# Two attention chunks turned by VectorE instead of TensorE, and an ordered start of the x sums, in a fused RetNet and GELU kernel on Trainium2

## The chip, the cores and the metric

The kernel runs on one core of a Trainium2 chip. Five engines work side by side, each through its own list of instructions in order: TensorE (PE), VectorE (DVE), ScalarE (ACT), GpSimd (POOL) and SyncE (SP). Here SP only issues loads and a few stores, POOL computes and issues transfers of its own, and all transfers share 16 DMA engines. The metric is the device time of one execution in microseconds, and a lower one is better. "Span" is the time from the first to the last instruction of the one execution that was profiled.

## What is computed

```python
def _attn_ref(q, k, v):                       # 4 batches, 8 heads, 768 steps, head size 64
    gamma = 1.0 - 2.0 ** (-5.0 - np.arange(H, dtype=np.float32))
    scale = 1.0 / np.sqrt(D)
    for t in range(S):
        state = gamma[None, :, None, None] * state + np.einsum('bhd,bhe->bhde', k[:, :, t], v[:, :, t])
        y[:, :, t] = scale * np.einsum('bhd,bhde->bhe', q[:, :, t], state)
    return y

def _moe_ref(x, w_in, w_out):                 # 3072 x 512, 512 x 2048, 2048 x 512
    h = x @ w_in
    g = h * (1.0 / (1.0 + np.exp(-1.702 * h)))
    return (g @ w_out).astype(np.float32)
```

The attention's output, heads side by side, is the x of the two products. The two weights come as float64 and everything is computed in float32.

## The kernel before

**Blocks.** The attention is cut into chunks of 64 steps. One "chunk" j covers two batches at once, one in each half of the 128 partitions, so there are 12 chunks for each pair of batches and 24 in all. Four chunks make a block of 512 tokens, and there are six blocks, 0 to 5. A block goes through the first product (up, L405 to L426 for blocks 0 and 1, L463 from block 2 on), GELU on ACT, and the second product (down, L670, or down49, L551). From block 2 on, the first product uses sums of x and of the weights that save multiplications.

**One chunk.** `load` (L124) fetches q, k and v. `turn` (L238) transposes q and k. `attend` (L279) writes the matmuls on PE: the inner products of chunk j into the tile pa, and for an earlier chunk f the state's update (also in pa), the part that comes from the state, and the part within the chunk (both in py). pa and py exist once each in PSUM. `masked` (L314) multiplies the inner products with the decay mask on DVE, `decay` (L261) scales k, `aged` (L349) scales the old state, `updated` (L360) adds the new part, `by_state` (L319) and `output` (L331) write x, in block 1 into X1.

**Two ways to turn.** Chunks 0 to 7 (`j < 2 * CB`) are loaded plainly, by two DMAs of 128 KB for each of q, k and v, and turned by PE: 16 matmuls against a unit matrix (L248), which ACT copies from PSUM (L259). Their decays and agings are done head by head on ACT (L270, L355). Chunks from 8 on are loaded as squares: eight DMAs of 32 KB for each of q and k (L154), which put 32 x 32 blocks in place so that one transpose on DVE (L251) for each of q and k finishes the work. They also need k and v as they are, in four DMAs of 64 KB each (L140). Their decays and agings are single instructions on POOL (L272, L357). The two ways lay heads out differently over the halves of the partitions. So `halves_anew` (L791) once rewrites the mask, the decays and the state between chunk 7 and chunk 8; it is called from `late_loads` (L786), the first loads for chunks 8 and 9.

**The raw weights.** Each of the 16 weight pieces w0 to w15 arrives as two DMAs of 512 KB (L177, "w5a", "w5b") in one of three raw buffers (L166), taken in turn: w7 waits until w4 is converted, and so on. Conversion is one instruction on ACT (`start`, "abs", L204), three on DVE (`half`) and three more (`rest`). W0 to w7 serve the first product, w8 to w15 the second.

**The order.** Up to the end of block 1's first product the order is written by hand, as a list of names (L844 to L861). The list interleaves loads ("q6"), turns, steps ("step6-5" is `attend(6, 5)`), conversions, the units of block 0's first product ("up0.0.3": token half 0, weight piece 3), those of block 1 ("up1.8"), and their GELUs ("gate"). PE follows it to the letter, and so does every instruction made under `pin` or `keep_in_program_order`, on its own engine and against other such instructions. Instructions that are not pinned are placed by a scheduler. That holds for most of POOL's work.

**Around the block boundaries.** `sums_x` (L437) makes four differences of x in place on POOL: X4 = X2 − X0, X6 = X3 − X2, X5 = X3 − X4 and X2 = X1 − X5. It is called once in each of blocks 1 to 4 for the block that follows (L908). The first product of the next block wants X0, X1, X5, X4, X6, X3 and X2, in this order. Block 1's results go through `put` (L681): DVE adds into a tile o, of which there are two, and POOL issues its transfer to DRAM (L684, pinned). In the later blocks POOL does four additions per tile first (L600 to L603) and then issues it (L604).

Of the kernel before, what the change touches and what calls it, by code (L numbers as in the profile page):

```python
# [13 lines left out]
P = 128  # L14
# [14 lines left out]
def kernel(  # L29
# [32 lines left out]
    B, H, S, D = q.shape  # L62
# [56 lines left out]
        return tc.keep_in_program_order(i) if ordered[0] else i  # L119


    QKV = {}

    def load(j, what="qkv"):  # L124

        b, c = j // NC * 2, j % NC
        rows = slice(c * D, (c + 1) * D)
        keep = tc.keep_in_program_order if j < 2 * CB else lambda i: i  # L130

        def plain(name, src, tag, bufs, engine=sp):
            t = two.tile([P, H, D], F32, name=name + "_in", tag=tag, bufs=bufs)
            QKV[name, j] = t
            for i in range(2):
                if j < 2 * CB:
                    keep(engine.dma_start(t[i * D:(i + 1) * D], src[b + i, :, rows, :].rearrange("h p d -> p h d")))  # L137
                else:
                    for r in range(2):
                        keep(engine.dma_start(t[r * D:(r + 1) * D, i * HP:(i + 1) * HP],  # L140
                                              src[b + i, r * HP:(r + 1) * HP, rows, :].rearrange("h p d -> p h d")))

        if j < 2 * CB:
            if "q" in what:
                plain("q", q, "q_sq", 2)
            if "k" in what:
                plain("kn", k, "k_sq", 2, sp if j else act)
        elif "q" in what:
            for name, src in (("q", q), ("k", k)):
                t = two.tile([P, H, D // C4, C4], F32, name=name + "_sq")  # L150
                for r0 in range(0, P, C4):
                    for n in range(D // C4):
                        t0 = c * D + n * C4
                        tc.keep_in_program_order(sp.dma_start(  # L154
                            t[r0:r0 + C4, :, n], src[b + r0 // D, :, t0:t0 + C4, r0 % D:r0 % D + C4]
                            .rearrange("h p d -> p h d")))
                QKV[name, j] = t
        if "v" in what:
            if j >= 2 * CB and c < NC - 1:
                plain("kn", k, "kn", 1)  # L160
            plain("v", v, "v", 2)

# [65 lines left out]
    def home(j, name):  # L228

        at = ["qT", "kT", "kd", "at"].index(name)  # L230
        shape = [[HP, P] if j < 2 * CB else [H, D]] * 2 + [[H, D], [2, HP, D]]
        shape = shape[at]
        if j >= 2 * CB:
            return one.tile([P] + shape, F32, name=name, tag=name, bufs=[2, 1, 1, 2][at])
        t = G[:, at, j % 2 * 2:j % 2 * 2 + 2].rearrange("p s t -> p (s t)")
        return t.rearrange("p (a b c) -> p a b c", a=2, b=HP) if at == 3 else t.rearrange("p (a b) -> p a b", a=shape[0])

    def turn(j):  # L238

        QT[j], KT[j] = home(j, "qT"), home(j, "kT")  # L240
        if j < 2 * CB:

            x = QKV.pop(("q", j)), QKV["kn", j]
            TURNED[j] = p = [ps.tile([P, HP, P], F32, name="pt", tag="y") for i in range(2)]
            for n in (1, 0) if j else (0, 1):
                for s in range(HP):
                    for r in range(2):
                        pe.matmul(p[n][HALF[r], s, :], x[n][:, HP * r + s, :], ident, start=True, stop=True)  # L248
        else:
            for t, name in ((QT[j], "q"), (KT[j], "k")):  # L250
                tc.keep_in_program_order(dve.transpose(  # L251
                    t.rearrange("p h t -> p (h t)"), QKV.pop((name, j)).rearrange("p h n d -> p (h n d)")))
        if 2 * CB <= j < NCH - 2:
            load(j + 2, "qk")
# [6 lines left out]
    def decay(j):  # L261

        if j % NC == NC - 1:
            return
        KD[j] = home(j, "kd")
        x = QKV["kn", j]
        if j < 2 * CB:

            for h in range(H):
                pin(act.activation(KD[j][:, h], x[:, h], AF.Copy, scale=cold[:, H + h:H + h + 1]))  # L270
        else:
            pool.tensor_mul(KD[j].rearrange("p (i s) d -> p i s d", i=2), x.rearrange("p (i s) d -> p i s d", i=2),  # L272
                            cold[:, None, H:H + HP, None].to_broadcast([P, 2, HP, D]))

    def by_half(t, j):

        return t.rearrange("p s (w t) -> p w s t" if j < 2 * CB else "p (w s) t -> p w s t", w=2)

    def attend(j, f=None):  # L279

# [7 lines left out]
        if f is not None:  # L288
# [17 lines left out]
            for s2 in range(2):  # L306
                for u in range(2):
                    for w, o in TWO:
                        s = 2 * s2 + o
                        pe.matmul(py[HALF[o], w, 0, 2 * u + s2 if f < 2 * CB else 2 * s2 + u, :],  # L310
                                  vn[HALF[w], HP * u + s, :], a[HALF[w], u, s, :], start=True, stop=True)
            PU[f], PY[f] = pa[:, :, 1], py

    def masked(j):  # L314
        AT[j] = home(j, "at")
        pin(dve.tensor_mul(AT[j], PA.pop(j)[:, :, 0],
                           mask if j < 2 * CB else mask[:, 0:1].to_broadcast([P, 2, HP, D])))

    def by_state(f):  # L319

        if f < 2 * CB:
            SHARE[f] = tmp = two.tile([P, 2, 4, D], F32, name="tmp", bufs=1)
            pin(dve.tensor_mul(tmp.rearrange("p i a t -> p i (a t)").rearrange("p i (r t) -> p i r t", r=2),
                               PY[f][:, :, 1].rearrange("p r (i s) t -> p i r (s t)", i=2),
                               rowd.rearrange("p (r s) t -> p r (s t)", r=2)[:, None].to_broadcast([P, 2, 2, P])))
        else:
            SHARE[f] = tmp = two.tile([P, 4, 2, D], F32, name="tmp", bufs=1)
            pin(dve.tensor_mul(tmp.rearrange("p a i t -> p i a t"), PY[f][:, :, 1],
                               rowd[:, None].to_broadcast([P, 2, HP, D])))

    def output(f):  # L331
# [1 line left out]
        th, t0 = f % CB // 2, f % 2 * D  # L333
        x = (X1 if f // CB == 1 else X)[:, 2 * th:2 * th + 2]
        y = PY.pop(f)[:, :, 0]
        if f < 2 * CB:
            x = x.rearrange("p r s (i t) -> p (r s) i t", i=2)[:, :, :, t0:t0 + D]
            y = y.rearrange("p i a t -> p a i t")
            b = "p i a t -> p a i t"
# [2 lines left out]
            b = "p (r s) i t -> p r (s i) t"  # L342
        if c:
            tmp = SHARE.pop(f)
            pin(dve.tensor_add(x, y, tmp.rearrange(b) if f < 2 * CB else tmp.rearrange(b, r=2)))  # L345
        else:
            pin(act.activation(x, y, AF.Copy))

    def aged(f):  # L349

        c = f % NC
        old, new = state[c % 2], state[(c + 1) % 2]
        if f < 2 * CB:
            for s in range(HP):
                pin(act.activation(new[:, :, s], old[:, :, s], AF.Copy, scale=whole[:, s:s + 1]))  # L355
        else:
# [78 lines left out]
        pool.tensor_sub(w[2], w[1], w[5])  # L435

    def sums_x():  # L437
        pool.tensor_sub(X[:, 4], X[:, 2], X[:, 0])
        pool.tensor_sub(X[:, 6], X[:, 3], X[:, 2])
        pool.tensor_sub(X[:, 5], X[:, 3], X[:, 4])  # L440
        pool.tensor_sub(X[:, 2], X[:, 1], X[:, 5])
# [344 lines left out]
    def late_loads():  # L786
        load(2 * CB, "qkv")
        load(2 * CB + 1, "qk")
        halves_anew()

    def halves_anew():  # L791

# [1 line left out]
                                        ap=[[0, P], [1, H]]))  # L794
        pool.tensor_copy(mask[HALF[1], 0], mask[HALF[1], 1])
        pool.tensor_copy(cold[HALF[1], H:H + HP], cold[HALF[1], H + HP:2 * H])
        old, new = state[2 * CB % NC % 2], state[(2 * CB + 1) % NC % 2]
        for u in range(2):
            pool.dma_start(new[HALF[1 - u], u], old[HALF[u], 1 - u])
        for u in range(2):  # L800
# [5 lines left out]

        "mask": lambda: pin(dve.tensor_mul(m3, products["rows"], cold[:, 0:H, None].to_broadcast([P, H, D]))),
        "causal": causal, "rows": rows,
        "rowd": lay_rowd, "whole": lay_whole, "late_loads": late_loads,
        "warm": keep_warm}  # L810
    for j in range(2 * CB):
        for name in "qkv":
# [31 lines left out]
    for name in """  # L844
# [2 lines left out]
        aged1 masked1 turned2 v2 rest0a abs2 q3 step-1 updated1 state1 decay2 aged2 step2 q4 x1 half2 decay3 w3b  # L847
        w3a up0.0.0 masked2 turn3 k4 step-2 v3 q5 rest2 k5 gate0.0.0 turned3 updated2 state2 step3 up0.0.2
        masked3 abs3 half3 x2 rest3 turn4 w1b step-3 aged3 gate0.0.2 turned4 state3 w1a w5b updated3 v5 decay4
        k6 abs1 x3 q6 turn5 half1 up0.0.3 turned5 up0.1.2 step4 aged4 w5a rest1 v4 gate0.0.3 decay5 w6a masked4  # L850
        turn6 gate0.1.2 abs5 w6b step5-4 half5 rest5 up0.0.1 updated4 turned6 k7 abs6 state4 gate0.0.1 w4b
        up0.1.1 half6 aged5 w8a up0.0.5 rest6 masked5 decay6 w4a q7 up0.1.5 gate0.1.1 x4 gate0.0.5 abs4 step6-5
        w8b half4 gate0.1.5 state5 updated5 turn7 turned7 aged6 abs8 w9b up0.1.6 gate0.1.6 x5 v6 masked6 step7-6
        v7 w9a decay7 up0.1.0 rest4 w7a masked7 abs9 updated6 state6 x6 w7b half8 step-7 state7 up0.1.4
        gate0.1.4 abs7 x7 up1.8 rest8 half7 up1.5 gate1.8 w11a rest7 half9 up1.4 gate1.4 w10b w10a w11b up0.0.7
        gate0.1.0 up1.0 gate0.0.7 rest9 up1.3 gate1.0 abs10 w12a gate1.5 gate1.3 up1.2 gate1.2 w12b up1.6
        gate1.6 abs11 up1.9 gate1.9 half11 rest11 up1.11 up0.0.4 up0.1.7 abs12 w14b half10 gate0.0.4 rest10
        aged7 up0.0.6 gate1.11 updated7 up1.10 gate0.1.7 w14a half12 gate0.0.6 abs14 half14 w13a gate1.10 rest12
        w13b up1.7 gate1.7 up1.12 up1.13 rest14 gate1.13 abs13 half13 gate1.12 w15a up1.15 gate1.15 w15b
        late_loads up1.14 abs15 up0.1.3 half15 rest13 up1.1 gate1.14 rest15 gate0.1.3 gate1.1  # L860
    """.split():  # L861
        works[name]()
    ordered[0] = False
# [92 lines left out]
```

## Time and profile before

| what | value |
|---|---|
| median of three runs | 671.96 us (671.05 to 672.71) |
| span of the profiled execution | 671.8 us |
| mean granted PE clock | 0.992 |
| PE busy in 0 to 84 us, 84 to 168 us | 73.75 us, 84.00 us |
| DMA share in 0 to 84 us, 84 to 168 us | 0.94, 0.33 |
| turn 6 and turn 7 on PE, start | 52.77 us, 73.38 us |
| squares of chunk 8 on SP, first issue | 143.98 us |
| first product of blocks 2, 3, 4, 5, start | 268.76, 373.82, 474.82, 575.46 us |

The page gives the busy time of each engine and its share of the span. In an order of time a line begins with the start and the duration in us, then the engine, the line of the kernel, the operation, what it writes and reads, how many were merged, and in brackets how long the engine idled before and what ended that. In the table of waits the columns are the total, the number of waits and the longest. Matmul durations overlap, so a block's cost on PE is taken from start to start. A float32 matmul leaves two records.

### The profile page before, as it was taken

What the parts mean: (1) busy time and instruction counts of PE and PEld (TensorE: products, weight loads), DVE (VectorE), ACT (ScalarE), POOL (GpSimd) and SP (SyncE); (2) the same over time, 40 slices, a digit from 0 to 9 for tenths busy, and PEclk for the clock granted to TensorE, in tenths of its full rate; (3) what the DMA queues carried; (4) which work ended last, traced back from release to release, by engine and by line L of the source; (5) the groups of instructions that cost most, each with busy time, mean ns of one, the idle gap of its engine ahead of it and who ended that gap; (6) DMA issues with size and microseconds to landing.
All of it is one profiled execution on the core that took longest, in us unless ns stands there. A gap on an engine that the chain in (4) does not pass through costs nothing.

```text
span 671.8 us, 15330 instructions
## 1 busy us (share of the span) xinstructions
PE 654.5 (97%) x6502; PEld 568.5 (85%) x6502; DVE 432.8 (64%) x614; ACT 157.0 (23%) x313; POOL 169.8 (25%) x192
## 2 busy tenths in 40 slices
PE   6799999999999999899999999999999999999997
PEld 4688865746888888788999988999888999988997
DVE  3697881869845775275996264997254995254965
ACT  5665512322000000233210233110233210233110
POOL 3000000010168416200255700254800255500000
PEclk9799999999999999899999999999999999999999
DMA  9979833333403446345287662276572153602142
GB/s 181 223 192 230 205 97 118 108 107 47 76 4 138 161 109 163 89 141 204 63 182 175 200 154 95 65 170 173 128 234 98 57 151 112 247 4 95 53 152 96
DMA packets 143781, 88.98 MB, mean 132 GB/s; under 512 B 129472, under 2 KB 130752, under 8 KB 142688
## 3 DMA queue, kind: packets, MB, share of 16 engines
q1 hardware_dynamic: 134224, 45.97, 30.2%
q0 software_dynamic: 7184, 40.78, 17.2%
q10 hardware_dynamic: 2304, 1.25, 0.6%
q8 instruction: 51, 0.84, 0.5%
q14 instruction: 18, 0.15, 0.1%
HBM read 72.37 MB, written 15.47 MB: 131 GB/s over the span
## 4 chain that ended last, share of the span: by engine, by line
PE 88%; DMA 5%; DVE 3%; POOL 2%; issue 1%; SPq 1%; ACT 0%; ACTq 0%; POOLq 0%; DVEq 0%
PE pq L574 26%; PE px L470 16%; PE py L470 12%; PE pd L707 10%; PE ph L425 8%; PE ph L412 8%; DMA kn_in<-in_k_dram 2%; DMA W2D<-X 2%; PE pt L248 2%; PE pa L287 2%; PE pa L295 2%; PE py L310 2%; PE py L304 1%; DMA v_in<-in_v_dram 1%; SPq L137 1%
## 5 line engine op out<-in xcount | busy, mean ns | idle before, releaser
L574 PE MATMUL pq<-W,G 128*128 128x128 f32 x672 | 80.2, 276 | 0.0
L574 PEld LDWEIGHTS pq<-W,G 128*128 128x128 f32 x672 | 77.6, 192 | 0.6
L543 POOL DMA_DIRECT2D ring<-W2D x28 | 15.4, 552 | 230.7 <-PE px L470 120.9
L470 PE MATMUL px<-X,W1A 128*128 128x256 f32 x256 | 61.0, 384 | 2.4 <-ACT p L477 2.1
L470 PE MATMUL px<-X,W1B 128*128 128x256 f32 x256 | 59.8, 379 | 0.0
L574 PE MATMUL pq<-ring,own 128*128 128x128 f32 x448 | 59.8, 276 | 0.0
L470 PEld LDWEIGHTS px<-X,W1A 128*128 128x128 f32 x256 | 48.7, 192 | 9.7 <-issue 2.5
L574 PEld LDWEIGHTS pq<-ring,own 128*128 128x128 f32 x448 | 54.5, 192 | 0.4
L470 PEld LDWEIGHTS px<-X,W1B 128*128 128x128 f32 x256 | 48.5, 190 | 6.7
L707 PE MATMUL pd<-W,G 128*128 128x256 f32 x224 | 49.6, 381 | 0.0
L707 PEld LDWEIGHTS pd<-W,G 128*128 128x128 f32 x224 | 42.2, 190 | 5.9
L470 PE MATMUL py<-X,W1A 128*128 128x256 f32 x192 | 46.1, 384 | 0.0
L470 PE MATMUL py<-X,W1B 128*128 128x256 f32 x192 | 45.4, 379 | 0.0
L391 ACT ACTIVATE G<-G 128x512 f32<-128x512 f32 x48 | 30.2, 630 | 51.0 <-DVE G L480 32.3
L470 PEld LDWEIGHTS py<-X,W1A 128*128 128x128 f32 x192 | 37.2, 194 | 5.3
L470 PEld LDWEIGHTS py<-X,W1B 128*128 128x128 f32 x192 | 36.5, 190 | 5.0
L488 DVE TENSOR_TENSOR t<-py,u 128x512 f32<-128x512 f32 x16 | 11.1, 692 | 34.6 <-PE py L470 34.6
L477 ACT ACTIVATE p<-px 128x512 f32<-128x512 f32 x16 | 9.6, 597 | 97.8 <-PE px L470 86.8
L412 PE MATMUL ph<-X,W1A 128*128 128x256 f32 x128 | 29.1, 383 | 1.1 <-DVE X L345 1.1
L574 PE MATMUL pq<-W,own 128*128 128x128 f32 x224 | 29.6, 275 | 0.0
L574 PE MATMUL pq<-ring,G 128*128 128x128 f32 x224 | 29.6, 275 | 0.0
L502 DVE TENSOR_TENSOR G<-G 128x512 f32<-128x512 f32 (+2 forms) x24 | 12.3, 513 | 25.7 <-ACT G L391 25.7
(203 smaller groups left out, 1174.5 us busy)
## 6 DMA issues: line engine op xcount, KB each, us to landing
ring<-W2D POOLq DMA_DIRECT2D x28, 768.0 KB, 5.1
W1B<-W1D POOLq DMA_DIRECT2D x6, 1792.0 KB, 9.4
W<-in_moe_w_in_dram SPq DMA_DIRECT2D x12, 512.0 KB, 6.1
W<-in_moe_w_out_dram SPq DMA_DIRECT2D x10, 512.0 KB, 4.8
out_dram<-o POOLq DMA_DIRECT2D x20, 256.0 KB, 3.0
v_in<-in_v_dram SPq DMA_DIRECT2D x64, 64.0 KB, 3.5
q_sq<-in_q_dram SPq DMA_DIRECT2D x128, 32.0 KB, 2.2
k_sq<-in_k_dram SPq DMA_DIRECT2D x128, 32.0 KB, 2.3
```

The costliest lines, as they stand in the source:

```text
L248: pe.matmul(p[n][HALF[r], s, :], x[n][:, HP * r + s, :], ident, start=True, stop=True)
L287: pe.matmul(pa[HALF[w], u, 0, s, :], kt[HALF[u], w, s, :], qt[HALF[u], w, s, :], start=True, stop=True)
L295: pe.matmul(pa[HALF[u], w, 1, s, :], kd[HALF[w], HP * u + s, :], vn[HALF[w], HP * u + s, :], start=True, stop=True)
L310: pe.matmul(py[HALF[o], w, 0, 2 * u + s2 if f < 2 * CB else 2 * s2 + u, :], vn[HALF[w], HP * u + s, :], a[HALF[w], u, s, :], start=True, s ...
L391: pin(act.activation(g, h[:, i], AF.Gelu_apprx_sigmoid))
L412: pe.matmul(h[:, ab], w, X[:, 2 * th + c // 2, c % 2, :], start=(ab == 0 and c == 0), stop=(c == 3), skip_group_check=True)
L425: pe.matmul(h, w, X1[:, c // 2:4:2, c % 2, :], start=(c == 0), stop=(c == 3))
L470: pe.matmul(acc[:, u, :], t[:, q1 + u, sa, c, :], X[:, sb, c, :], start=(start and u == 0 and c == 0), stop=(stop and c == 1), skip_group_ ...
L502: dve.tensor_sub(q[0][1], q[0][0], q[0][1])
L543: pool.dma_start(c, W2D[i])
L574: pe.matmul(p0[:, j, :], a[:, d], w[:, d], start=(new and j == 0 and d == 0), stop=(d == NP // 2 - 1), skip_group_check=True)
L707: pe.matmul(p0[:, n, :], g1(m, p, sa)[:, n * P:(n + 1) * P], W2[:, sb, p, :], start=(new and p == 0 and n == 0), stop=(last and p == NP - ...
```

## The change

The bound between the two ways to turn is now a constant NEW = 6 in place of `2 * CB` = 8. Chunks 6 and 7 are loaded as squares and turned by DVE, and their decays and agings go to POOL. The tiles for them still lie in G as before. `halves_anew` becomes an entry of the list, "anew", and runs between chunk 5 and chunk 6. The list is written anew from "k6" on: the plain loads of q and k of chunks 6 and 7 go, their squares ("q6", "q7", which load k too) come after w8 and w9, and chunks 6 and 7 are spread over the rest of block 0's first product, all of whose units now come before block 1's. The loads of w4, w7, w8 and the later pieces move with them. In `sums_x` the first difference, X4, is kept in program order.

As it is built, PE has turn 6 and turn 7 taken out, and step 5's inner products directly behind step 4's. SP issues, from chunk 5's v on: w5, v of chunk 4, w6, w4, w8, the squares of chunk 6, its k and v, w7, w9, the squares of chunk 7, its k and v, k and v of chunk 8, w11, w10. POOL issues at the start of block 2: X6, the two waiting outputs, X4, X5, X2. In each of the boundaries to blocks 3, 4 and 5, where it had X4, X6, L602, X5, L603, X2 and the output, it now has X6, L602, L603, the output, X4, X5, X2.

```diff
+    NEW = 6
 ...
-        if j < 2 * CB:
+        if j < NEW:
             if "q" in what:
                 plain("q", q, "q_sq", 2)
 ...
-            if j >= 2 * CB and c < NC - 1:
+            if j >= NEW and c < NC - 1:
                 plain("kn", k, "kn", 1)
 ...
     def turn(j):
         QT[j], KT[j] = home(j, "qT"), home(j, "kT")
-        if j < 2 * CB:
+        if j < NEW:
 ...
     def sums_x():
-        pool.tensor_sub(X[:, 4], X[:, 2], X[:, 0])
+        tc.keep_in_program_order(pool.tensor_sub(X[:, 4], X[:, 2], X[:, 0]))
         pool.tensor_sub(X[:, 6], X[:, 3], X[:, 2])
 ...
     def late_loads():
         load(2 * CB, "qkv")
         load(2 * CB + 1, "qk")
-        halves_anew()
 ...
-        old, new = state[2 * CB % NC % 2], state[(2 * CB + 1) % NC % 2]
+        old, new = state[NEW % NC % 2], state[(NEW + 1) % NC % 2]
 ...
-        k6 abs1 x3 q6 turn5 half1 up0.0.3 turned5 up0.1.2 step4 aged4 w5a rest1 v4 gate0.0.3 decay5 w6a masked4
-        turn6 gate0.1.2 abs5 w6b step5-4 half5 rest5 up0.0.1 updated4 turned6 k7 abs6 state4 gate0.0.1 w4b
-        up0.1.1 half6 aged5 w8a up0.0.5 rest6 masked5 decay6 w4a q7 up0.1.5 gate0.1.1 x4 gate0.0.5 abs4 step6-5
-        w8b half4 gate0.1.5 state5 updated5 turn7 turned7 aged6 abs8 w9b up0.1.6 gate0.1.6 x5 v6 masked6 step7-6
-        v7 w9a decay7 up0.1.0 rest4 w7a masked7 abs9 updated6 state6 x6 w7b half8 step-7 state7 up0.1.4
+        abs1 x3 turn5 half1 up0.0.3 turned5 up0.1.2 step4 aged4 w5a rest1 v4 gate0.0.3 decay5 w6a masked4
+        gate0.1.2 abs5 w6b step5-4 half5 rest5 up0.0.1 updated4 abs6 state4 gate0.0.1 w4b
+        up0.1.1 half6 aged5 w4a up0.0.5 rest6 masked5 up0.1.5 gate0.1.1 x4 gate0.0.5 abs4 step-5 w8b w8a
+        half4 gate0.1.5 state5 updated5 anew q6 up0.1.6 x5 rest4 gate0.1.6 abs8 v6 up0.0.6 w7b w7a half8
+        turn6 gate0.0.6 up0.1.0 abs7 half7 gate0.1.0 w9b w9a up0.1.4 q7 gate0.1.4 decay6 step6 masked6 rest7 up0.0.4 v7
+        gate0.0.4 turn7 up0.1.3 gate0.1.3 aged6 step7-6 masked7 updated6 decay7 abs9 state6 x6 up0.0.7 rest8 gate0.0.7
+        w11a w11b step-7 state7 x7 half9 w10b w10a up0.1.7 rest9 gate0.1.7 abs11 half11 up1.8 gate1.8
 ...
```

More of the change, by code (lines that the diff above doesn't have):

```diff
@@ L230, in home @@
         at = ["qT", "kT", "kd", "at"].index(name)
-        shape = [[HP, P] if j < 2 * CB else [H, D]] * 2 + [[H, D], [2, HP, D]]
+        shape = [[HP, P] if j < NEW else [H, D]] * 2 + [[H, D], [2, HP, D]]
         shape = shape[at]
@@ L240, in turn @@
         QT[j], KT[j] = home(j, "qT"), home(j, "kT")
-        if j < 2 * CB:
+        if j < NEW:
             x = QKV.pop(("q", j)), QKV["kn", j]
@@ L266, in decay @@
         x = QKV["kn", j]
-        if j < 2 * CB:
+        if j < NEW:
             for h in range(H):
@@ L275, in by_half @@
     def by_half(t, j):
-        return t.rearrange("p s (w t) -> p w s t" if j < 2 * CB else "p (w s) t -> p w s t", w=2)
+        return t.rearrange("p s (w t) -> p w s t" if j < NEW else "p (w s) t -> p w s t", w=2)
     def attend(j, f=None):
@@ L309, in attend @@
                         s = 2 * s2 + o
-                        pe.matmul(py[HALF[o], w, 0, 2 * u + s2 if f < 2 * CB else 2 * s2 + u, :],
+                        pe.matmul(py[HALF[o], w, 0, 2 * u + s2 if f < NEW else 2 * s2 + u, :],
                                   vn[HALF[w], HP * u + s, :], a[HALF[w], u, s, :], start=True, stop=True)
@@ L316, in masked @@
         pin(dve.tensor_mul(AT[j], PA.pop(j)[:, :, 0],
-                           mask if j < 2 * CB else mask[:, 0:1].to_broadcast([P, 2, HP, D])))
+                           mask if j < NEW else mask[:, 0:1].to_broadcast([P, 2, HP, D])))
     def by_state(f):
-        if f < 2 * CB:
+        if f < NEW:
             SHARE[f] = tmp = two.tile([P, 2, 4, D], F32, name="tmp", bufs=1)
@@ L335, in output @@
         y = PY.pop(f)[:, :, 0]
-        if f < 2 * CB:
+        if f < NEW:
             x = x.rearrange("p r s (i t) -> p (r s) i t", i=2)[:, :, :, t0:t0 + D]
@@ L344, in output @@
             tmp = SHARE.pop(f)
-            pin(dve.tensor_add(x, y, tmp.rearrange(b) if f < 2 * CB else tmp.rearrange(b, r=2)))
+            pin(dve.tensor_add(x, y, tmp.rearrange(b) if f < NEW else tmp.rearrange(b, r=2)))
         else:
@@ L352, in aged @@
         old, new = state[c % 2], state[(c + 1) % 2]
-        if f < 2 * CB:
+        if f < NEW:
             for s in range(HP):
@@ L808 @@
         "causal": causal, "rows": rows,
-        "rowd": lay_rowd, "whole": lay_whole, "late_loads": late_loads,
+        "rowd": lay_rowd, "whole": lay_whole, "late_loads": late_loads, "anew": halves_anew,
         "warm": keep_warm}
@@ L854 @@
-        v7 w9a decay7 up0.1.0 rest4 w7a masked7 abs9 updated6 state6 x6 w7b half8 step-7 state7 up0.1.4
[L855 to L858, printed above, removed]
@@ L859 @@
-        w13b up1.7 gate1.7 up1.12 up1.13 rest14 gate1.13 abs13 half13 gate1.12 w15a up1.15 gate1.15 w15b
-        late_loads up1.14 abs15 up0.1.3 half15 rest13 up1.1 gate1.14 rest15 gate0.1.3 gate1.1
+        abs1 x3 turn5 half1 up0.0.3 turned5 up0.1.2 step4 aged4 w5a rest1 v4 gate0.0.3 decay5 w6a masked4
+        gate0.1.2 abs5 w6b step5-4 half5 rest5 up0.0.1 updated4 abs6 state4 gate0.0.1 w4b
+        up0.1.1 half6 aged5 w4a up0.0.5 rest6 masked5 up0.1.5 gate0.1.1 x4 gate0.0.5 abs4 step-5 w8b w8a
@@ new lines @@
+        half4 gate0.1.5 state5 updated5 anew q6 up0.1.6 x5 rest4 gate0.1.6 abs8 v6 up0.0.6 w7b w7a half8
+        turn6 gate0.0.6 up0.1.0 abs7 half7 gate0.1.0 w9b w9a up0.1.4 q7 gate0.1.4 decay6 step6 masked6 rest7 up0.0.4 v7
+        gate0.0.4 turn7 up0.1.3 gate0.1.3 aged6 step7-6 masked7 updated6 decay7 abs9 state6 x6 up0.0.7 rest8 gate0.0.7
+        w11a w11b step-7 state7 x7 half9 w10b w10a up0.1.7 rest9 gate0.1.7 abs11 half11 up1.8 gate1.8
+        w12a w12b rest11 up1.5 gate1.5 up1.4 gate1.4 abs10 half10 up1.0 gate1.0 rest10 up1.3 gate1.3 abs12
@@ L861 @@
+        aged7 updated7 up1.2 gate1.2 w14b w14a half12 up1.6 gate1.6 rest12 up1.9 gate1.9 abs14 half14 w13a w13b
+        up1.11 gate1.11 rest14 up1.10 gate1.10 abs13 half13 w15a w15b up1.7 gate1.7 rest13 abs15 half15 up1.12
+        gate1.12 late_loads up1.13 gate1.13 rest15 up1.15 gate1.15 up1.14 gate1.14 up1.1 gate1.1
     """.split():
```

## The prediction

> **What bounds the kernel now.** I read the page's busy times first, then the order of time on TensorE (PE), then its waits.
>
> ```profile
> PE 654.5 (97%) x6502; PEld 568.5 (85%) x6502; DVE 432.8 (64%) x614; ACT 157.0 (23%) x313; POOL 169.8 (25%) x192
> ```
>
> PE is the bound: idle 671.8 − 654.5 = 17.3 us, of which 84 − 73.75 = 10.25 us lie in the first 84 us. So an instruction taken off PE is time won, unless a wait fills its place. In order of time PE shows the two blocks to be removed (turn 6 and turn 7) and what stands around them:
>
> ```profile
> 52.15 0.69 PE L287 MATMUL pa<-G 64*64 64x64 f32 x32
> 52.77 1.09 PE L248 MATMUL pt<-ident,kn_in 128*64 128x128 f32 x16
> 53.70 1.04 PE L248 MATMUL pt<-ident,q_in 128*64 128x128 f32 x16
> 54.67 0.69 PE L287 MATMUL pa<-G 64*64 64x64 f32 x32
> ...
> 73.38 1.09 PE L248 MATMUL pt<-ident,kn_in 128*64 128x128 f32 x16
> 74.30 1.04 PE L248 MATMUL pt<-ident,q_in 128*64 128x128 f32 x16
> 75.28 3.72 PE L412 MATMUL ph<-X,W1B 128*128 128x256 f32 x16
> ```
>
> From start to start each turn holds PE for 1.90 us. PE's waits after the opening are few; two of them concern the x sums:
>
> ```profile
> PE px L470 <- ACT p L477: 2.1, 1, 2.1
> ...
> PE px L470 <- POOL X L440: 0.3, 1, 0.3
> ```
>
> The first is at the start of block 2. The chain of waits in order of time:
>
> ```profile
> 268.82 0.51 POOL X L441
> ...
> 270.04 2.75 DMA out_dram<-o
> ...
> 272.91 0.70 DVE o L683
> ...
> 273.72 0.61 ACT p L477
> ...
> 274.46 2.93 PE px L470 x8
> 277.39 2.45 PE py L470 x8
> 279.84 1.73 PE px L470 x8
> ```
>
> POOL does four x sums (265.04 to 270.04), then issues block 1's two waiting outputs; the third output buffer is the first one again, so DVE, ACT and PE wait for that transfer. The next two products take 2.93 and 2.45 us instead of 1.73. The second wait is at the start of block 4 (POOL's order of time):
>
> ```profile
> 474.29 1.27 POOL L438 TENSOR_TENSOR X<-X 128x512 f32<-128x512 f32 x1
> 475.52 1.26 POOL L439 TENSOR_TENSOR X<-X 128x512 f32<-128x512 f32 x1
> 476.74 0.73 POOL L602 TENSOR_TENSOR o<-o 128x256 f32<-128x256 f32 x1
> 477.43 1.26 POOL L440 TENSOR_TENSOR X<-X 128x512 f32<-128x512 f32 x1
> ```
>
> PE's third product there wants X5 (L440) at 476.55 + 1.73 = 478.28; it starts at 478.75.
>
> [...] A square's rows are 32 floats, 128 B; the trace has 66 GB/s at a DMA share of 0.43 for squares against 209 at 0.59 for weights. [...]
>
> **Part 1: PE loses turns 6 and 7.** 2 x 1.90 = 3.80 us. The evacuations (4 x 0.60), decays (16 x 0.25) and agings (8 x 0.32) that leave ACT, 9 us, win nothing: ACT is 23% busy. POOL gets two decays and two agings at 1.04 us each; it stands idle from 81 to 132 us. DVE gets 4 x 0.70 us and has 15.64 us of idling at 103 us; only the last pair can count (below). State and mask are laid out anew at about 74 us instead of 132 (1.36 issue, 3.15 landing, 1.50 copies, so ready at 80), with four product units before the first reader. Nothing.
>
> **Part 2: where turn 6 stood.** Step 5's first matmul writes the same single PSUM buffer (pa) as step 4's, and waits for DVE's mask read of it, 52.91 to 53.60. Turn 6 hid that. Now step 5 starts at 53.66 instead of 52.67. In return v of chunk 4 is issued some 5 us earlier (the k and q loads ahead of it are gone), which ends the 0.33 us wait for v at 55.8. From step 4 to the next unit: before 57.34 − 52.15 = 5.19; after 0.52 + 0.99 + 0.52 + 1.54 = 3.57. Gain 1.62 of the 1.90, so 0.28 given back. The bounds are 0.2 and 0.7.
>
> **Part 3: do the squares of chunk 7 come in time?** Per chunk, SP now issues 16 squares (3.86 us per 8 in the trace) and 8 halves of k and v (0.65 each): 13 us instead of 6 x 0.64 = 3.8. And each SP load waits for the one eight before it. PE in the new order: 53.66 + 2.06 = 55.72; four units of 3.50 give 69.72; step 5's rest 1.56; four units, 85.28; step 6's 0.57; two units, 92.85: here step 7 wants turn 7. DVE: x5 ends at 73.3, rest4 3.2 later at 76.5, which frees the raw buffer for w7. SP has finished chunk 6's squares, k and v by 75 (from 61 on), so w7 is issued at 76.5; before, the same pair took 5.6 us in the median, so the second lands near 83.4. W9 follows and lands at 86 to 88.5 (4.5 to 5.1 us for such loads, queued). The eighth q square waits for that, the k squares then take 3.6 us of issue and 2.0 to landing: 93 (91.5 to 95). One transpose, 0.70, and PE starts at 93.8: a wait of 1.0 (0 to 2.5). I take 1.0. Behind it in SP's queue stand k and v of chunk 7, landed by 99, wanted at 99.4 by step 7's own products; then k and v of chunk 8 (waiting for POOL's decay) and w11, whose reader has 6 us to spare. Step 7's x is done by DVE at 102.4, two us before the first unit of block 1 wants it. DVE has converted w15 some 7 us before block 0's second product. Nothing more here.
>
> **Part 4: the x sums.** At the start of block 2 the new order on POOL is X6, both outputs, X4, X5, X2. The first output goes at 266.3 instead of 270.04, lands at 269.0, DVE is done at 269.8 and ACT at 271.2, before PE's third product at 272.2. X5 is ready at 270.3. The fifth product moves from 279.68 to 275.67: a gain of 4.01 (2.08 wait, 1.93 slow clock and its edges). But the pin sits in a function that all four boundaries call. In blocks 3 to 5 POOL now does X6, L602, L603, the output, and only then X4 and X5. Such a triple takes 466.10 − 463.48 = 2.62 us in the trace. Block 4: 475.52 + 2.62 + 1.23 + 1.26 = 480.63, PE at 480.70 instead of 478.75: 1.95 lost, a wait of 2.42. That is longer than the one that halved the clock, so I add a slow window, 3.4 us at half, 1.7 (bounds 0 and 1.9). Block 3: L602 waits for DVE until 372.1; X5 ends at 377.24 against 377.27 wanted: 0.05 (0 to 0.5). Block 5 wants X5 at 578.92, 6.4 us after L440 ended there: nothing.
>
> **Sum.** −3.80 + 0.28 + 1.0 − 4.01 + 0.05 + 1.95 + 1.7 = −2.8. On its own span of 671.8 that is 669.0; the three timed runs (671.05 to 672.71) have their median 0.16 above it. I take 669.2.
>
> **Rivals.** (a) As worked out: 669.2, own range 668.0 to 670.7. (b) No slow clock at block 4: [...] For it: only one gap of such a size is in this trace. Against: the gap is longer than that one. 669.2 − 1.7 = 667.5. (c) Nor any wait for squares or X5, because POOL or SP runs ahead of my reckoning: 671.96 − 3.80 + 0.28 − 4.01 = 664.4; against it stands POOL's order, fixed in the program. (d) Weights and squares share the queue more slowly, as the longest landing of a raw load, 8.7 us, allows: squares 2 to 3 us later, 671 to 673. (e) Slower than before: the SP queue starves steps 6 and 7. Place: SP between w7 and v of chunk 7. PE loses a microsecond for each that the last k square of chunk 7 lands after 93[...]. Above 671.96 + 2.0 it needs 674.0 − 669.2 = 4.8 us more, so a landing after 96. For it: 48 small loads where 12 stood, each waiting for one eight back. Against: SP's queue was waiting, not issuing, for most of that stretch before. 676. That the change does not do what it says is part of (a): its pin reaches three more boundaries than the one named.
>
> **How the numbers follow.** A change of 0.3%, 2.0 us, is about what can be told from none. Chances: (a) 0.45, (b) 0.20, (c) 0.10, (d) 0.13, (e) 0.12. Faster takes (b), (c) and 0.32 of (a): 0.62. Same takes the rest of (a) and nearly all of (d): 0.25. Slower: (e) and a remnant, 0.13. The range leaves out most of (e) and the far end of (c): 665.5 to 673.5.
>
> **What would show it.** Right: no transposing pt matmuls after turn 5; PE waits about 1 us for DVE's mask at 53 us; no wait for ACT p at block 2 and clock 1.00 there; a PE wait of about 2.4 us for X5 at block 4, with clock 0.50 behind it. Wrong: no wait at block 4, PE waits for transposed q or k of over 2 us, or for X4 to X6 at block 2.

## The result and the profile after

The changed kernel takes 667.6 us in the median of six runs (666.5 to 670.03), beside 671.53 us for six runs of the kernel before (669.46 to 672.71). The ratio is 0.9946, interval 0.9923 to 0.997: 3.6 us faster, with 2.0 and 5.2 us as the ends. (Ratios here are worked out from all runs of the two kernels, so they are not quite the quotients of the medians, which lie 3.9 us apart.) One of the 22 runs of the list alone took 3841 us and is left out of its ratio. All line numbers up to the launch code are one higher than before (the x sums are L439 to L442, the products L471, the pt turns L249).

PE has lost the work it was to lose, 64 matmul records, as the page's first section shows.

```profile
PE 648.7 (97%) x6438; PEld 563.2 (85%) x6438; DVE 435.9 (65%) x618; ACT 148.7 (22%) x285; POOL 174.9 (26%) x196
```

The profiled execution has a span of 666.4 us, 5.4 less than the one before. Laying PE's starts of the same work side by side shows where these 5.4 us lie:

| stretch on PE | before, us | after, us | difference |
|---|---|---|---|
| start of the span to the first product unit (28.20, 26.99) | 28.20 | 26.99 | −1.21 |
| first product unit to step 4 (52.15, 50.94) | 23.95 | 23.95 | 0 |
| step 4 to the first down product (161.92, 160.56) | 109.77 | 109.62 | −0.15 |
| first down product to block 2 (268.76, 267.40) | 106.84 | 106.84 | 0 |
| block 2 to block 3 (373.82, 367.93) | 105.06 | 100.53 | −4.53 |
| block 3 to block 4 (474.82, 469.66) | 101.00 | 101.73 | +0.73 |
| block 4 to block 5 (575.46, 570.30) | 100.64 | 100.64 | 0 |
| block 5 to the end | 96.34 | 96.10 | −0.24 |

The first row lies ahead of anything that was changed: ten profiled executions of this study have their first product unit anywhere from 26.99 to 28.20 us. In the kernel before the clock there was 0.50 from 19.3 to 26.1 us, 6.83 us, in the changed one from 19.8 to 23.2, 3.41 us, two lengths that both come in other executions with the old order as with the new. So of the 5.4 us some 1.2 are luck. Of the 4.53 us between blocks 2 and 3, the fifth product accounts for 4.01, and 0.25 is an issue gap at 352.5 us that the kernel before alone has there. The stretch that lost two turns of 1.90 us each has gained almost nothing in this execution. PE's order of time there shows three idle stretches around the places of the turns:

```profile
50.94 0.69 PE L288 MATMUL pa<-G 64*64 64x64 f32 x32
52.54 0.69 PE L288 MATMUL pa<-G 64*64 64x64 f32 x32 [0.91 <-DVE G L317]
53.02 0.68 PE L296 MATMUL pa<-v_in,G 64*64 64x64 f32 x32
53.49 0.44 PE L305 MATMUL py<-G,state 64*64 64x64 f32 x15
54.99 0.50 PE L305 MATMUL py<-G,state 64*64 64x64 f32 x17 [1.07 <-issue]
55.28 0.68 PE L311 MATMUL py<-G,v_in 64*64 64x64 f32 x32
55.89 7.17 PE L413 MATMUL ph<-X,W1A 128*128 128x256 f32 x32
...
94.84 0.69 PE L288 MATMUL pa<-G 64*64 64x64 f32 x32 [1.57 <-DVE G L252]
```

Step 5 (52.54) waits for DVE's mask. At 53.9 us a second gap cuts one group of 32 small matmuls in two; "issue" means that nothing in the profile released it. Step 7 (94.84) waits for DVE's transposes of chunk 7. SP's order of time shows why:

```profile
76.63 1.57 SPq L178 DMA_DIRECT2D W<-in_moe_w_in_dram  x2
78.25 0.94 SPq L178 DMA_DIRECT2D W<-in_moe_w_out_dram  x2
79.23 8.78 SPq L155 DMA_DIRECT2D q_sq<-in_q_dram  x8
88.11 3.86 SPq L155 DMA_DIRECT2D k_sq<-in_k_dram  x8
```

DVE's order of time:

```profile
90.03 0.70 DVE L252 STREAM_TRANSPOSE G<-q_sq 128x512 f32<-128x512 f32 x1
93.98 0.71 DVE L252 STREAM_TRANSPOSE G<-k_sq 128x512 f32<-128x512 f32 x1 [3.25 <-DMA k_sq<-in_k_dram]
```

The k squares take the 3.86 us that eight issues cost; the q squares ahead of them take 8.78. Each load waits on SP for the one eight places back; for the last two q squares these are the halves of w9, which landed at 85.57 and 87.69, and the two squares were issued at 85.59 and 87.70.

The start of block 2 is where the time came from. POOL's order of time there:

```profile
262.88 1.26 POOL L440 TENSOR_TENSOR X<-X 128x512 f32<-128x512 f32 x1
264.09 1.51 POOL L685 DMA_DIRECT2D out_dram<-o  x2
265.62 1.28 POOL L439 TENSOR_TENSOR X<-X 128x512 f32<-128x512 f32 x1
266.97 1.27 POOL L441 TENSOR_TENSOR X<-X 128x512 f32<-128x512 f32 x1
```

The chain of waits over the same stretch (start, duration, what):

```profile
267.56 1.73 PE px L471 x8
269.29 1.73 PE py L471 x8
271.02 1.73 PE px L471 x8
272.75 1.73 PE py L471 x8
274.47 1.73 PE px L471 x8
```

Nothing but products, each 1.73 us long, where before stood POOL, the output's transfer, DVE, ACT and a product of 2.93 us. The granted clock is 1.00 throughout.

At block 4 the prediction had put a loss of 3.65 us. It isn't there. POOL's order of time:

```profile
465.06 1.04 POOL L273 TENSOR_TENSOR kd<-kn_in,cold 128x512 f32<-128x512 f32 x1 [4.24 <-DMA kn_in<-in_k_dram]
466.06 1.04 POOL L358 TENSOR_TENSOR state<-state,whole_h 128x512 f32<-128x512 f32 x1
467.06 1.27 POOL L440 TENSOR_TENSOR X<-X 128x512 f32<-128x512 f32 x1
...
472.27 1.27 POOL L441 TENSOR_TENSOR X<-X 128x512 f32<-128x512 f32 x1
```

PE's third product, in its order of time:

```profile
473.59 1.99 PE L471 MATMUL px<-X,W1A 128*128 128x256 f32 x8 [0.31 <-POOL X L441]
```

POOL does what was predicted, X6, the triple, X4, X5. But it begins 2.60 us ahead of the block's first product (467.06 against 469.66), where before it began 0.53 us ahead. The wait of 0.31 us is the same as before. The +0.73 us between blocks 3 and 4 is another matter: 0.40 of it is an issue gap at 441 us, and the rest was not traced.

### The profile page after: what moved, and what is told of

Same layout as the page of the kernel before. It is cut to its first block, busy times and chain, and to the rows that moved or that the text cites. A ratio compares the mean times of both kernels' runs of the same rounds, so it can differ in the third digit from the quotient of the medians.

```text
span 666.4 us, 15234 instructions
## 1 busy us (share of the span) xinstructions
PE 648.7 (97%) x6438; PEld 563.2 (85%) x6438; DVE 435.9 (65%) x618; ACT 148.7 (22%) x285; POOL 174.9 (26%) x196
## 4 chain that ended last, share of the span: by engine, by line
PE 88%; DMA 4%; DVE 3%; POOL 2%; SPq 1%; issue 1%; ACT 0%; ACTq 0%; POOLq 0%; DVEq 0%
PE pq L575 24%; PE px L471 16%; PE pd L708 13%; PE py L471 12%; PE ph L426 8%; PE ph L413 5%; DMA kn_in<-in_k_dram 2%; PE pa L288 2%; PE pt L249 2%; PE py L311 2%; PE py L305 2%; PE pa L296 2%; DMA W<-in_moe_w_out_dram 1%; SPq L155 1%; DVE W1A L456 0%
## 5 line engine op out<-in xcount | busy, mean ns | idle before, releaser
L575 PE MATMUL pq<-W,G 128*128 128x128 f32 x672 | 80.5, 276 | 0.4 <-issue 0.4
L575 PEld LDWEIGHTS pq<-W,G 128*128 128x128 f32 x672 | 77.6, 192 | 1.2 <-issue 0.6
L471 PE MATMUL px<-X,W1A 128*128 128x256 f32 x256 | 60.0, 380 | 0.3 <-POOL X L441 0.3
L471 PE MATMUL px<-X,W1B 128*128 128x256 f32 x256 | 59.8, 379 | 0.0
L575 PE MATMUL pq<-ring,own 128*128 128x128 f32 x448 | 59.8, 276 | 0.0
L575 PEld LDWEIGHTS pq<-ring,own 128*128 128x128 f32 x448 | 54.5, 192 | 0.4
L471 PEld LDWEIGHTS px<-X,W1A 128*128 128x128 f32 x256 | 48.2, 190 | 7.3 <-POOL X L441 0.9
L471 PEld LDWEIGHTS px<-X,W1B 128*128 128x128 f32 x256 | 48.5, 190 | 6.7
L471 PE MATMUL py<-X,W1A 128*128 128x256 f32 x192 | 45.4, 379 | 0.0
L471 PE MATMUL py<-X,W1B 128*128 128x256 f32 x192 | 45.4, 379 | 0.0
L471 PEld LDWEIGHTS py<-X,W1A 128*128 128x128 f32 x192 | 36.5, 190 | 5.0
L471 PEld LDWEIGHTS py<-X,W1B 128*128 128x128 f32 x192 | 36.5, 190 | 5.0
L575 PE MATMUL pq<-W,own 128*128 128x128 f32 x224 | 29.6, 275 | 0.0
L575 PE MATMUL pq<-ring,G 128*128 128x128 f32 x224 | 29.6, 275 | 0.0
```

The lines of the kernel that those rows point to most:

```text
L471: pe.matmul(acc[:, u, :], t[:, q1 + u, sa, c, :], X[:, sb, c, :], start=(start and u == 0 and c == 0), stop=(stop and c == 1), skip_group_ ...
L575: pe.matmul(p0[:, j, :], a[:, d], w[:, d], start=(new and j == 0 and d == 0), stop=(d == NP // 2 - 1), skip_group_check=True)
```

## The experiments

The table of stretches suggests one theory and the prediction's sum another. Theory P takes the profile at its word: nearly all of the gain is the pin's, at block 2, and the list brings almost nothing. Rival L has it the other way, as the first three parts of the sum do: the list brings most, the pin little. Theory S came up after the first results: the price of the pin at block 4 is real, but whether it is paid depends on when the k load of chunk 20 lands.

**The list alone.**

```diff
-        tc.keep_in_program_order(pool.tensor_sub(X[:, 4], X[:, 2], X[:, 0]))
+        pool.tensor_sub(X[:, 4], X[:, 2], X[:, 0])
```

> The kernel after, with X4 unpinned again, so the new list alone. Theory P (the pin brought the gain, and the new list paid its 3.8 us on TensorE back in waits): within 1 us of before, so about 0.999 of it; at the start of block 2 ACT p waits for the output again, TensorE idles about 2 us there and the clock drops to 0.50. Rival L (the list brings 3 us as worked out, and the pin only the rest): 0.995 to 0.996.

Measured: 669.11 us, ratio to before 0.9966 (0.9953 to 0.9979), which is 2.3 us (1.4 to 3.2) of 672.14. The wait at block 2 is back, in PE's order of time:

```profile
272.20 1.96 PE L471 MATMUL px<-X,W1A 128*128 128x256 f32 x8 [1.89 <-ACT p L478]
```

The clock stayed at 1.00 behind it. Step 5's wait is 0.91 us again, step 7's is 1.11, and there is no issue gap at 53 us. The gain lies between what the two theories gave: the list does bring something, against P, whose 0.999 lies outside the interval; L's 0.995 to 0.996 overlaps it. The gain fits the 2.52 us of the prediction's first three parts.

**The pin alone**, in the kernel before: the same line, the other way round.

> The kernel before, with X4 pinned, so the pin alone. Theory P: 0.994 (4.0 us less), if the boundary to block 4 waits no longer than 0.5 us; with the 2.4 us wait that I had worked out for block 4 (1.95 more idling and up to 1.7 of slow clock) only 1 to 2 us less, 0.997 to 0.999. Rival L: 0.998 or more, since most of the gain would be the list's. The trace tells by the start of X4 on POOL against the first product of block 4.

Measured: 669.61 us, ratio 0.9966 (0.9952 to 0.998), again 2.3 us (1.3 to 3.2). P's 0.994 lies outside this interval, and L's 0.998 is its end. So the two parts bring about the same, P does not hold and L only at the edge of the intervals, and 2.3 + 2.3 = 4.6 lies within the 2.0 to 5.2 us of both together. The wait for ACT's p is gone, and the wait for X5 is 0.2 us: no loss at block 4, with the pin in place. What the span of this execution lost was elsewhere, an issue gap in a stretch that this kernel shares with the one before, in PE's order of time:

```profile
26.95 0.45 PE L287 MATMUL pa<-G 64*64 64x64 f32 x12 [2.74 <-issue]
```

The granted clock was 0.50 from 27.8 to 31.2 us, behind it.

**Chunk 7's squares ahead of w9.**

```diff
-        turn6 gate0.0.6 up0.1.0 abs7 half7 gate0.1.0 w9b w9a up0.1.4 q7 gate0.1.4 decay6 step6 masked6 rest7 up0.0.4 v7
+        turn6 gate0.0.6 up0.1.0 abs7 half7 gate0.1.0 q7 w9b w9a up0.1.4 gate0.1.4 decay6 step6 masked6 rest7 up0.0.4 v7
```

> The kernel after, with chunk 7's squares issued ahead of the two loads of w9. Theory P: the 1.57 us that TensorE waits for the transposed k of chunk 7 is SP's queue (the eighth q square waits for w9), so it falls to under 0.3 and the time by 1.3 to 1.6 us, 0.9917 to 0.993 of before. Rival (the squares themselves are slow, or DVE is): the wait stays over 1 us and the time is that of the kernel after, 0.9946.

Measured: 667.17 us, ratio 0.9934 (0.9915 to 0.9952). The expected 0.9917 to 0.993 and the rival's 0.9946 both lie within the interval, so the trace has to decide: step 7's wait is gone, and SP's order of time shows why:

```profile
77.14 6.06 SPq L155 DMA_DIRECT2D q_sq<-in_q_dram  x8
83.30 3.86 SPq L155 DMA_DIRECT2D k_sq<-in_k_dram  x8
```

The k squares are issued at 83.30 instead of 88.11. The k squares stand behind the q squares in SP's list: the eight q issues took 8.78 us in the changed kernel and 6.06 here, and the eight k issues behind them 3.86 in both. In this execution PE waited for X5 at block 3 instead, with the pinned order (its order of time):

```profile
370.19 1.99 PE L471 MATMUL px<-X,W1A 128*128 128x256 f32 x8 [0.94 <-POOL X L441]
```

**One product unit between step 4 and step 5.**

```diff
-        gate0.1.2 abs5 w6b step5-4 half5 rest5 up0.0.1 updated4 abs6 state4 gate0.0.1 w4b
+        gate0.1.2 abs5 w6b up0.0.1 step5-4 half5 rest5 updated4 abs6 state4 gate0.0.1 w4b
```

> The kernel after, with one unit of block 0's first product put between step 4 and step 5 on TensorE, where turn 6 stood. Theory P: the 0.91 us wait for DVE's mask goes, 0.6 to 0.9 us less than the kernel after, 0.993 to 0.9937 of before. [...]

Measured: 666.96 us, ratio 0.9934 (0.991 to 0.9959). The wait for the mask is gone; step 7's wait is 1.36 us, and a wait of 0.63 us for ACT at 85.11 (the x buffer) came. The issue gap is neither at step 5 nor elsewhere in this stretch; but four executions that kept the changed kernel's order there lack it too, so this run does not decide what it was. Neither of these two edits can be told from the changed kernel by its time, since a microsecond lies within the intervals; what each did to its wait is read from the trace.

**The kernel before, profiled once more.**

> The kernel before, unchanged, a second profile of it. Its first profile shows POOL beginning block 4's x sums (L438) 0.53 us ahead of that block's first product; five profiles of changed kernels show 2.4 to 3.0 us. Theory S (the start follows chunk 20's k load, whose landing shifts by 2 us between executions whatever the order): 2.4 to 3.0 us ahead here too, and no PE wait for X5 there or one under 0.4 us. Rival K (the old order sets it): 0.5 us ahead again, with the 0.3 us wait.

PE's order of time at block 2:

```profile
273.86 1.97 PE L470 MATMUL px<-X,W1A 128*128 128x256 f32 x8 [2.71 <-ACT p L477]
```

POOL's at block 4:

```profile
469.16 1.04 POOL L272 TENSOR_TENSOR kd<-kn_in,cold 128x512 f32<-128x512 f32 x1 [4.27 <-DMA kn_in<-in_k_dram]
470.15 1.04 POOL L357 TENSOR_TENSOR state<-state,whole_h 128x512 f32<-128x512 f32 x1
471.15 1.27 POOL L438 TENSOR_TENSOR X<-X 128x512 f32<-128x512 f32 x1
```

Block 4 starts at 473.73, so POOL's sums began 2.58 us ahead, with no wait for X5 there. The same kernel had 0.53 in its first profile. Theory S holds against rival K: the start is no property of the order. At block 2 the wait was 2.71 us, longer than the 2.08 of the first profile, and yet the clock was 1.00 behind it.

**A late start at block 4, with the pin and without.** To have the late start on demand, POOL decays chunk 20's k three times over, with the same values, in both kernels.

```diff
-            pool.tensor_mul(KD[j].rearrange("p (i s) d -> p i s d", i=2), x.rearrange("p (i s) d -> p i s d", i=2),
-                            cold[:, None, H:H + HP, None].to_broadcast([P, 2, HP, D]))
+            for _ in range(3 if j == 20 else 1):
+                pool.tensor_mul(KD[j].rearrange("p (i s) d -> p i s d", i=2), x.rearrange("p (i s) d -> p i s d", i=2),
+                                cold[:, None, H:H + HP, None].to_broadcast([P, 2, HP, D]))
```

> The changed kernel with the decay of chunk 20's k (L273) done three times over on POOL instead of once, with the same values, so that all four x sums of block 4 start 2.08 us later. Theory S (the step on the pin at block 4 was right in its mechanism, its start alone was wrong): X5 is ready about 475.6 where PE's third product wants it at 473.3, a PE wait of 2.1 to 2.5 us, and perhaps a clock of 0.50 for 3.4 us behind it; 2.1 to 4.0 us slower than the changed kernel (ratio to before 0.997 to 1.000). Rival N (the pin costs nothing at block 4 wherever POOL starts): PE wait under 0.5 us, ratio 0.993 to 0.995.

The second kernel frees X4 at this one boundary.

```diff
-        tc.keep_in_program_order(pool.tensor_sub(X[:, 4], X[:, 2], X[:, 0]))
+        first = pool.tensor_sub(X[:, 4], X[:, 2], X[:, 0])
+        if m != 3:
+            tc.keep_in_program_order(first)
```

> As the one with the decay done three times over, but X4 is pinned at the other three boundaries only and free at block 4. Theory S: X5 comes ahead of the output there, a PE wait of 0 to 0.5 us at block 4, clock 1.00, and 1.6 to 3.5 us faster than the same with the pin (ratio to before 0.993 to 0.996). Rival N: no difference between the two beyond their intervals.

Measured: with the pin 671.97 us, ratio 1.0001 (0.9985 to 1.0017); without it 667.62 us, ratio 0.9924 (0.99 to 0.9949). The pin at this boundary costs 4.35 us between the medians (5.2 by the ratios) once POOL starts late, all that the change had won. That is more than the 1.6 to 3.5 us expected. The kernel with the pin, in PE's order of time:

```profile
473.39 1.89 PE L472 MATMUL py<-X,W1A 128*128 128x256 f32 x8
479.21 3.78 PE L472 MATMUL px<-X,W1A 128*128 128x256 f32 x8 [3.93 <-POOL X L442]
482.79 2.61 PE L472 MATMUL py<-X,W1A 128*128 128x256 f32 x8
```

Two windows of the same kernel (after the stretch and its length, busy time of PE, PEld, DVE, ACT and POOL, then PE's clock, the DMA share and GB/s):

```profile
478.00:480.00 2.00, 0.79 (x2) 0.70 (x3) 0.00 (x0) 0.00 (x0) 1.92 (x2) 0.50 0.51 107
480.00:482.00 2.00, 2.00 (x7) 1.55 (x6) 0.00 (x0) 0.00 (x0) 1.78 (x4) 0.50 0.45 103
```

And the one without it, in PE's order of time:

```profile
476.21 1.99 PE L474 MATMUL px<-X,W1A 128*128 128x256 f32 x8 [1.30 <-POOL X L444]
```

A wait of 3.93 us and two products that take 479.21 to 485.24, 6.03 us instead of 3.46, so 2.57 us of slow clock; against 1.30 us and a clock of 1.00. Both waits are larger than expected (2.1 to 2.5, and 0 to 0.5). The reason is in the same traces: beyond the two extra decays, chunk 20's k came late by itself, its decay starting 3.06 and 3.65 us ahead of block 4 where the changed kernel had 465.06 against 469.66, 4.60 us. And both profiled executions were the slowest of their kernels (676.16 us of 22 runs, 670.7 of 8), so the two waits are bad cases rather than typical ones; what the pin costs on the whole is in the medians.

**Three edits together**: both edits to the list, and the pin for block 2's boundary alone.

```diff
-    def sums_x():
-        tc.keep_in_program_order(pool.tensor_sub(X[:, 4], X[:, 2], X[:, 0]))
+    def sums_x(m):
+        first = pool.tensor_sub(X[:, 4], X[:, 2], X[:, 0])
+        if m == 1:
+            tc.keep_in_program_order(first)
```

> The changed kernel with three edits: one product unit put between the two halves of step 5, chunk 7's q squares issued ahead of w9, and the pin on X4 at block 2's boundary alone. If the waits are what the trace says, the 0.9 us for the mask at 53 us, the 1.6 us for the turned k of chunk 7 and 0.1 to 0.4 us of waits for X5 at blocks 3 and 4 go, and about 0.6 us for the x buffer at 85 us may come: 1.5 to 2.5 us faster than the changed kernel, ratio to before 0.990 to 0.9925. Rival: the two waits share one cause further up SP's queue and only the larger one is won, ratio 0.993.

Measured: 665.22 us, ratio to before 0.9887 (0.9862 to 0.9911), clear of the changed kernel's 0.9923 to 0.997 and a little better than the 0.990 to 0.9925 expected. Its PE waits for nothing at 52 us, nothing at 92 us and for no x sum; what is left are waits in the opening, issue gaps, a wait of 0.3 us in the second product that the kernel before has too, and a small new one, as its table of waits has them (in all, times, longest; line numbers are a little higher here):

```profile
PE pq L577 <- issue: 1.1, 1, 1.1
PE pa L288 <- issue: 0.9, 1, 0.9
...
PE ph L413 <- ACT X L392: 0.2, 1, 0.2
```

From step 4 to the first down product PE takes 157.87 − 51.60 = 106.27 us, 3.5 less than the 109.77 before. Nearly the whole 3.80 of the two turns is won there. How the gain in time divides among the three edits was not timed.

## Why the prediction was right, and where it was not

The forecast was 669.2 us, its range 665.5 to 673.5. The 667.6 us measured lies in the range and on the side named, but the sum of −2.8 came near −3.9 (3.6 by the ratio) with two of its terms far off, in opposite directions; that the total came so near is luck.

**Part 1, right.** No pt matmul stands behind turn 5, and 64 records are gone. Everything costed at nothing cost nothing: no wait for the new layout of state and mask, for ACT, or for x7, which DVE finished at 102.94 + 0.69 us.

**Part 2, right, with one thing beside it.** The wait for DVE's mask is 0.91 us. From step 4 to the next unit PE takes 3.62 us (53.08 to 56.70) and 3.63 us (51.45 to 55.08) in the two executions with the late start, against 3.57 predicted. In the profiled execution of the changed kernel it takes 4.95; the 1.07 us issue gap and a slower start behind it fell there, which none of the other four executions with this piece of the order shows. The DMA share was 0.95 at 52 to 54 us, and the last section has what else the records show of such gaps; no run tested the cause, and whether the gap comes as often in runs without a profiler can't be seen.

**Part 3, right in its mechanism, short in size.** SP held the squares behind w7 and w9, as worked out, and the last k square let DVE go at 93.98 instead of 93 (92.78 to 94.18 over the five executions with this order of loads). The wait at step 7 is 1.57 us where 1.0 was taken; over the five executions it is 0.96, 1.11, 1.36, 1.57 and 1.85, mean 1.37, within the bounds of 0 to 2.5. Not in the sum at all was what the new places of steps 6 and 7 cost on PE by themselves: cut apart, steps 5 to 7 take 1.56 + 0.62 + 2.02 + 1.56 = 5.76 us from start to start instead of 2.03 + 2.02 + 1.56 = 5.61, and the twelve product units around them 42.41 instead of 42.14 (their pieces from start to start, waits taken off). That is 0.15 + 0.27 = 0.42 us. This accounts for the profiled execution, where −0.15 us was left of the −3.80: 4.95 − (5.19 − 1.90) = 1.66 us at step 5, 1.57 at step 7 and 0.42. With 0.33 for part 2, the mean of 1.37 and these 0.42 the list comes to −3.80 + 2.12 = −1.7; timed alone it brought 2.3 (1.4 to 3.2).

**Part 4 at block 2: the mechanism right, the size only one of several.** POOL's order, its times and PE's undisturbed products came exactly as said. But the gain of 4.01 took 1.93 us of slow clock (0.50 from 275.3 to 278.7 us, 3.41 us, in the first profile) for a fixed part of the kernel before. The two other executions with the old order at that place waited 1.89 and 2.71 us at a clock of 1.00. In these traces the pin wins the wait each time and the slow clock once in three, and timed alone it brought 2.3 us, not 4.0.

**Part 4 at block 4: this step failed.** It set X5 at 475.52 + 2.62 + 1.23 + 1.26 on the time scale of one trace, and so took POOL's start, 0.53 us ahead of the block, for a constant. It isn't. The start follows the decay of chunk 20's k, which follows a load; over ten profiled executions that decay began 2.52 (the first profile), 3.06, 3.59, 3.65, 4.44, 4.57, 4.60, 4.69, 4.84 and 5.03 us ahead of the block's first product. The prediction was worked from the worst of the ten. In the changed kernel's execution the 2.07 us of earlier start took up the 1.95 of loss. The pair with the late start shows that the rest of the step was sound: at a late start the pin does bring a long wait for X5 and a clock of 0.50 behind it. Of the difference of the two waits, 3.93 − 1.30 = 2.63 us, the later start explains 3.65 − 3.06 = 0.59; the other 2.04 stand against the 1.95 of the forecast. The slow clock cost 2.57 us against 1.7, beyond the bound of 1.9. That a wait longer than 2.08 us would bring it was an estimate from one wait; the 2.71 us at block 2 of the second profile did not. The lateness of the decay is already there when SP issues its load: the last of its four parts was issued 5.66 to 6.41 us ahead of the block in the four executions with the latest decays, and 7.74 to 9.05 in the other six. What makes SP late there was not settled.

**Part 4 at block 3: the bound was too narrow.** The forecast was 0.05 us, with 0.5 as the most. With the pinned order PE did not wait for X5 there in three executions (the changed kernel, the pin alone, the later step 5), but 0.48, 0.94 and 1.02 us in three others.

**The rivals.** (b), 667.5, names the median measured, yet not the reason: not only the slow clock at block 4 was missing but the wait as well. (c) was right on X5 and wrong on the squares. (d) and (e) did not come: the k squares landed at 94, not at 95 or after 96 (the 96 of (e) counts 3.1 us of lateness behind 93 and 1.7 us of slow clock, an estimate from the 1.93 us at block 2).

Without its 3.70 us for blocks 3 and 4 the sum would have been −6.5; −3.6 was measured, with −5.2 as the far end. Of the 2.9 us between them, block 2's term accounts for 1.7 (4.01 in the sum, 2.3 timed): its slow clock was there in one of three executions. The rest lies within the intervals.

## What to carry to other kernels

A time read from one trace can be a point of a wide distribution where it hangs on a DMA's landing (chunk 20's decay began 2.52 to 5.03 us ahead of block 4): before a slack of half a microsecond decides a forecast, look at a second profile of the same kernel, or give both ends. A pin written into a function pins every caller; put on the one boundary that needs it, it keeps the gain without the risk at the others. Work taken off the bounding engine also took away the cover of small waits (0.91 us at step 5, 1.57 at step 7), and one product unit and one load moved by a few places gave that cover back; with the pin cut down to its one boundary they took the ratio from 0.9946 to 0.9887.

## What the runs showed of the hardware

In these traces the length of a gap did not tell whether the PE clock fell behind it. Gaps of 2.08 us (block 2, the first profile of the kernel before), 2.74 us (at 27 us, the pin alone) and 3.93 us (block 4, the late start with the pin) were followed by a clock of 0.50; so were two gaps of 0.82 and 1.44 us close together (24 to 27 us, the late start with the pin), behind which the mean clock was 0.72 from 28 to 32 us. Gaps of 1.89 us (the list alone) and 2.71 us (the second profile of the kernel before), both at block 2, were followed by a clock of 1.00. The clock stayed at 0.50 for 3.41 us behind the gap of 2.08 and for 3.4 us behind the one of 2.74; behind the one of 3.93 it was 0.50 from 478 to 482 us, as the windows in that experiment show. What sets these gaps apart was not shown: no run moved a gap on purpose, and the ends of matmuls in the traces are modelled.

PE also stopped at times in the middle of a group of like matmuls, with nothing in the profile that released it. Many of the places recur: the kernels with the new list all have such a gap at about 440 us, in the same group (L575 in the changed kernel; 0.40 to 1.51 us), both profiles of the kernel before have one at about 351 us in the same L310 group (0.25 and 0.82), and five of the ten executions have one at about 27 us, all ahead of the last 12 of the 32 matmuls of the same step (0.20 to 2.74). The length varies from execution to execution. The page of the changed kernel lists 50 DMA transfers of the kind "instruction" on queue q8, that of the kernel before 51, of 16 KB each. (The gaps of 0.30 and 0.31 us at about 15 us in these two executions stand ahead of a whole group and are another kind.) In the changed kernel's execution the gaps of 0.69, 1.07 and 0.40 us (up to 26.61, 54.99 and 441.00 us) ended 1.44, 1.51 and 1.28 us after one of these transfers had ended; in the first profile of the kernel before the gap of 0.25 us (up to 352.53 us) ended 1.33 us after one. That is a coincidence in time, four times over; no run varied these transfers, so the cause of the gaps is not shown.
